# Landmark sums of batch 1 taken from token-layout copies of q and k on TensorE, three subtractions moved to VectorE, and another written order for the first twelve slots

## The chip, the cores and the metric

The kernel runs on one core of a Trainium2 chip. The metric is the device time of one execution in microseconds. Of the kernel before, three timed runs took 854.84, 856.5 and 857.36 us (median 856.5 us); the one execution that was profiled took 852.74 us, of which the trace spans 850.7 us.

## The reference

Three stages follow one another. A Nyström attention over 4 batches, 8 heads, 576 tokens and head size 64; a gated layer on its 2304 x 512 output; and a second layer with a mish-like activation.

```python
q_lm = q.reshape(B, H, m, S // m, D).mean(axis=3)     # m = 32 landmarks, 18 tokens each
k_lm = k.reshape(B, H, m, S // m, D).mean(axis=3)
A, Bm, C = sm(q, k_lm), sm(q_lm, k_lm), sm(q_lm, k)   # scaled softmax rows
Z = Bm.T / (norm1(Bm) * norminf(Bm) + 1e-06)
for _ in range(6):
    Z = 2 * Z - Z @ Bm @ Z
x = A @ Z @ C @ v
...
x = ((x @ w_a) * (x @ w_b)) @ w_out                   # 512 -> 1536 -> 512
...
h = x @ w_in                                          # 512 -> 2048
out = (h * tanh(softplus(h))) @ w_out2
```

The weights arrive as 64-bit floats, and the kernel converts them to 32 bits itself. A landmark is needed as a sum over 18 consecutive tokens; the factor 1/18 is folded into the scale of the exponentials.

## The kernel before

Queries and keys are stored with the head dimension on the partitions (`kt`, `qt`: 128 partitions x 4 head pairs x 576 tokens). `lm_sum` (line 144) makes the landmark sums `kl` and `ql` with one VectorE `tensor_reduce` over two head pairs at a time, so four of them per batch.

For each batch the attention is a chain of small steps that `attention` holds by name: `kl`, `ql`, `sB` (landmark scores and softmax), `BB` and six `NS` (the iteration for Z), `sC0`/`sC1` (landmark queries against all keys, in two halves), `ET0`/`ET1` (transposes), `U` (times v), `M`, and `A0`/`A1`, `A0n`/`A1n` (queries against landmarks, softmax, and a split of the result `af` into a high part and a low part, both in `at`). Each step is a generator that pauses where it goes from one engine to another. The `NS` step asks TensorE, then ScalarE (a copy), then VectorE.

The first layer works in *slots*. A slot is one 128-wide block of hidden columns over 288 tokens: 6 products into one bank for `w_a`, 6 into the next for `w_b` (`ps_ab<-at,bm`, 12 matmul records per slot), a ScalarE copy `ta`, a VectorE product `tg`, and a split `g` on ScalarE and GpSimd. The weights in it are folded first: `fold` multiplies the attention's `MT` with `wab` and splits the result into `bm` (ScalarE copy, VectorE subtraction). The products with `w_out` (`o0` to `o7` in the order, `ps_o<-g,wo`) take 12 matmul records each.

Weight units are converted by `to_f32` (line 367): one ScalarE operation and four VectorE operations on 128 x 512 values. Units `c0` to `c3` give the `wab` for the first fold, `c4` to `c7` for the second, `c8` to `c11` are the first four of `w_out` (they have one more VectorE split, `wo<-f,wo`), `c12` to `c19` come after.

The order of the opening is written out by hand in `ORDER_1` (line 342): each word advances one generator by one pause; a word with `+` belongs to batch 1, a number is that many filler matmuls on an identity, `s0` to `s11` are the first twelve slots, `f0`, `f1`, `F0`, `F1` the folds of batches 0 and 1, `|` the point where banks are handed over. On VectorE, ScalarE and TensorE the words fix the order in which instructions stand; each engine then runs its line strictly in that order. From slot 12 on the order is made by the loops from line 749, which are not changed.

All loads stand in one queue, SP's, in program order. A load into a tile that is in use waits there for its readers. The keys of batch 1 go into the same buffer as those of batch 0 (`tag="kv"`, `bufs=1`), so their load waits until `sC1` of batch 0 has read it.

Of the kernel before, what the change touches and what calls it, by code (L numbers as in the profile page):

```python
# [17 lines left out]
LM = 32  # L18
# [10 lines left out]


@with_exitstack
def nystrom_moe_kernel(ctx: ExitStack, tc: tile.TileContext, q, k, v, w_a, w_b, w_out1, w_in2, w_out2, out):
    nc = tc.nc
    NT = B * S
    gp = nc.gpsimd
# [93 lines left out]
    PAIRS0 = {"sC0": "p3", "ET0": "bm", "ET1": "p3", "A0": "bm", "U": "p3"}  # L129
    PAIRS1 = {"ET0": "bm", "ET1": "bm"}  # L130

    def attention(ap, b, kt, qt, vt0=None):

        x = {}
        first = b == 0
# [2 lines left out]
        def sm(shape, nm, bufs=1, tag=None):  # L138
            return ap.tile(shape, F32, tag=tag or nm, bufs=bufs, name=nm)
# [164 lines left out]
        def An(r):  # L304
            ss, sa = x["ss", r], x["sa"][:, r]
            sa3 = sa.rearrange("p c (n l) -> p (c n) l", l=LM)
            ve.tensor_reduce(out=ss[:, :, 1], in_=sa3, axis=AX, op=ALU.add)
            yield
            ve.tensor_scalar(ss[:, :, 2], ss[:, :, 1], 1e-9, None, op0=ALU.add)
            ve.reciprocal(ss[:, :, 3], ss[:, :, 2])  # L310
            ve.tensor_tensor(sa3, sa3, ss[:, :, 3:4].to_broadcast([128, 18, LM]), op=ALU.mult)
            yield
            af = sm([128, 2, 288], "af")
            for c in range(2):
                ve.transpose(out=af[:, c], in_=sa[:, c])
            yield
            at = AT[b, r] = main.tile([128, 2, 2, S // 2], F32R, tag="AT", bufs=6, name="at")
            ac.activation(at[:, 0], af, AF.Copy)
            yield
            (ve if (b, r) == (0, 0) else gp).tensor_tensor(at[:, 1], af, at[:, 0].bitcast(F32), op=ALU.subtract)  # L320

        steps = {
            "kl": lambda: lm_sum(kt, "kl"), "ql": lambda: lm_sum(qt, "ql"), "sB": sB, "BB": BB, "NS": NS, "U": Uv, "M": M,
# [16 lines left out]

    N_UNITS, N_SLOTS = 20, 12
    ORDER_1 = """
        kl kl ql ql c0 sB sC0 sB c0 sB sC1 4 c1 sB sC0 BB 2 c2 sC1 BB c3 sC1 NS 2 c1 sC1 c2 c3 sC1 c0 c1 NS
        ET0 NS c2 c3 NS 2 ET0 c0 ET1 NS NS c4 c1 A0 ET1 c2 NS 1 c5 A0 U NS c6 NS A0 NS c7 c3 NS A0 NS U NS c0
        NS NS c1 NS NS c2 M A0n M A1 c3 A0n f0 A0n f0 +kl A0n f0 A0n +kl | s0 +ql s0 s0 s1 +ql s1 A1 A1 +sC0
        +sC1 +sC0 A1 +sC1 A1n A1n A1n +sC1 A1n s0 c4 +sC1 A1n s1 c5 c6 +sC1 +sB s1 +sB s0 +ET0 c7 s1 s0 c4 +sB
        s2 +ET0 +sB s1 s2 +ET1 c5 c6 +BB +ET1 c7 c4 s2 c8 +BB +U s2 c5 s2 +NS +U s2 s3 +NS +NS c6 +NS s3 c7 s3
        +NS +NS c4 +NS c5 +NS +NS c6 +NS c7 +NS +NS f1 s3 c8 s3 c8 s3 +NS c8 f1 c8 +NS c9 +NS f1 +NS c8 +NS s4
        c9 +M c9 s4 s4 c9 +M c9 s5 s4 c9 +A0 c8 s5 c9 s4 s5 c10 s4 +A0 s6 s5 F0 c10 s6 c10 s5 +A0 c11 s5 s6 F0
        s7 s6 +A0 c11 +A1 c11 s7 s6 c11 s7 c12 s6 c11 +A0n c11 c11 +A0n +A0n F0 +A0n +A0n s7 F1 c10 s7 c10 s7  # L350
        F1 s8 c12 c12 c10 F1 s8 s8 c10 s9 s8 c12 o0 s9 s8 c12 s8 +A1 c13 s9 +A1 o0 s10 o1 s9 s10 c13 +A1 c13
        s9 c13 c14 s10 s9 c13 o1 s11 s10 c14 s10 o2 c14 s11 s10 c14 c15 c14 s11 o2 c15 c15 o3 +A1n c15 c16
        +A1n o4 o3 c16 c16 o5 c15 o4 c17 +A1n c17 +A1n o6 c17 o5 c16 +A1n c16 o7 o6 s11 c17 s11 s11 c17 c18 o7
        c18 c18 c18 c18 c19 c19 c19 c19 c19
    """

    def stage(src, shape, early):
# [56 lines left out]
                        pass  # L414
                    self.prefetch()

    wab = {}
    wabd = [dram.tile([128, 2048], F32, name=f"wabd{g}") for g in range(6)]

    def wab_units(g):  # L420
        def conv(i, jj, st):
            if g not in wab:
                wab[g] = main.tile([128, 4, 2, 256], F32, tag="wab", bufs=3, name="wab")
            t = wab[g]
            yield from to_f32(t[:, 2 * jj:2 * jj + 2, i], st, True)
# [558 lines left out]
```

## Time and profile before

| | |
|---|---|
| three timed runs | 854.84, 856.5, 857.36 us |
| the profiled execution | 852.74 us, span of its trace 850.7 us |
| PE busy | 794.7 us (93%) |
| DVE busy | 565.8 us (67%) |
| ACT busy | 342.1 us (40%) |
| POOL busy | 153.2 us (18%) |

PE is TensorE's matmuls, PEld its weight loads, DVE is VectorE, ACT ScalarE, POOL GpSimd. The share of busy time is a mean over stages with different limits: in the first two slices of the page's strip (21 us each) PE is at five to six tenths, and from the fifth slice on at nine. DVE runs the other way, with eight and nine tenths at the start and three to four at the end.

An idle time in the trace is put down to the releaser that came last, shown as `[us <-releaser]` behind a row.

### The profile page before, as it was taken

Reading aid. Unit: us, or ns where it says so; the run is one execution under the profiler, and the core shown is the slowest. Engines: PE = TensorE matmul, PEld = TensorE weight load, DVE = VectorE, ACT = ScalarE, POOL = GpSimd, SP = SyncE. Lnnn points to the kernel's source line nnn. Section 1 sums busy time; section 2 is a strip of 40 time slices with the busy share of each in tenths; the row PEclk is TensorE's granted clock in tenths of the full one; section 3 lists DMA queues with packets and bytes.
Section 4 is the critical chain, followed back from the end, with each engine's and each line's share of the span. In section 5 each row is a group of like instructions: output and inputs, shape, how many; then the busy total and the mean of one; then the engine's idle time right before and its main releaser. Section 6 shows DMA issues by size and latency. Waiting matters only on the chain.

```text
span 850.7 us, 14559 instructions
## 1 busy us (share of the span) xinstructions
PE 794.7 (93%) x5802; PEld 691.9 (81%) x5802; DVE 565.8 (67%) x1027; ACT 342.1 (40%) x684; POOL 153.2 (18%) x144
## 2 busy tenths in 40 slices
PE   5666999999999999999988999999999999999997
PEld 4444887987887888787987898988988989988986
DVE  7899977895575488888985678768433347433433
ACT  3335454444323445444443444345332334332332
POOL 0011222222230232122234335320000000000000
PEclk9798899999999999999999899999999999999999
DMA  9736467458227338777376857788655445654501
GB/s 357 306 120 229 160 214 246 179 206 319 81 85 255 163 113 314 247 265 238 115 251 274 302 215 259 264 310 336 247 196 212 173 171 200 227 213 179 186 1 74
DMA packets 47891, 180.85 MB, mean 213 GB/s; under 512 B 4176, under 2 KB 12368, under 8 KB 38480
## 3 DMA queue, kind: packets, MB, share of 16 engines
q1 hardware_dynamic: 47824, 179.93, 58.9%
q8 instruction: 45, 0.74, 0.3%
q14 instruction: 22, 0.18, 0.1%
HBM read 126.44 MB, written 53.48 MB: 211 GB/s over the span
## 4 chain that ended last, share of the span: by engine, by line
PE 75%; DVE 14%; DMA 6%; issue 3%; ACT 2%; SPq 0%; POOL 0%; ACTq 0%; DVEq 0%
PE ps_ab L56 33%; PE ps_o L56 21%; PE ps_bm L56 11%; PE ps_at L56 10%; DVE f L56 5%; DMA kt<-in_k_dram 3%; DMA wi2d<-f 2%; DVE tg L56 1%; DVE f L378 1%; DVE bm L56 1%; DMA wo2d<-f 1%; DVE kl L56 1%; ACT f L374 1%; DVE x2acc L56 1%; DVE s L56 1%
## 5 line engine op out<-in xcount | busy, mean ns | idle before, releaser
L56 PE MATMUL ps_ab<-xc,wc 128*128 128x384 f32 x1008 | 201.7, 340 | 4.8 <-DVE u2s L56 3.1
L56 PE MATMUL ps_ab<-at,bm 128*128 128x288 f32 x1152 | 192.0, 307 | 13.4 <-DVE tg L56 6.9
L56 PEld LDWEIGHTS ps_ab<-at,bm 128*128 128x128 f32 x1152 | 165.4, 194 | 41.9 <-issue 11.8
L56 PEld LDWEIGHTS ps_ab<-xc,wc 128*128 128x128 f32 x1008 | 181.8, 189 | 16.9 <-DVE u2s L56 3.4
L56 PE MATMUL ps_o<-g,wo 128*128 128x288 f32 x1152 | 180.0, 298 | 3.1 <-DVE x2acc L56 2.1
L56 PEld LDWEIGHTS ps_o<-g,wo 128*128 128x128 f32 x1152 | 161.0, 188 | 15.4 <-issue 5.9
L519 POOL TENSOR_TENSOR g<-tg,g 128x288 fp32r<-128x288 f32 x96 | 87.1, 908 | 268.0 <-ACT g L56 268.0
L56 ACT ACTIVATE m<-c 128x384 f32<-128x384 f32 x96 | 50.2, 523 | 189.6 <-DVE c L56 189.5
L56 PE MATMUL ps_bm<-wo,g 128*128 128x512 f32 x288 | 95.5, 396 | 0.3 <-ACT g L56 0.3
L56 PE MATMUL ps_at<-wo,g 128*128 128x512 f32 x288 | 82.9, 395 | 0.0
L56 DVE TENSOR_TENSOR g<-m,g 128x384 fp32r<-128x384 f32 x96 | 66.7, 696 | 23.0 <-ACT g L56 23.0
L56 PE MATMUL ps_o<-wo,g 128*128 128x512 f32 x288 | 79.6, 393 | 0.0
L56 ACT ACTIVATE g<-tg 128x288 fp32r<-128x288 f32 x96 | 42.4, 442 | 79.9 <-DVE tg L56 79.7
L56 DVE SCALAR_TENSOR_TENSOR f<-stg,f 128x512 uint32<-128x512 uint32 x88 | 72.1, 823 | 1.6
L56 PEld LDWEIGHTS ps_at<-wo,g 128*128 128x128 f32 x288 | 54.3, 189 | 10.7
L56 DVE TENSOR_TENSOR tg<-ps_ab,ta 128x288 f32<-128x288 f32 x96 | 43.2, 451 | 29.7 <-PE ps_ab L56 21.9
L56 ACT ACTIVATE ta<-ps_ab 128x288 f32<-128x288 f32 x96 | 38.9, 405 | 57.4 <-PE ps_ab L56 56.9
L56 PEld LDWEIGHTS ps_o<-wo,g 128*128 128x128 f32 x288 | 53.6, 188 | 9.1
L56 PEld LDWEIGHTS ps_bm<-wo,g 128*128 128x128 f32 x288 | 53.7, 189 | 7.0 <-ACT g L56 0.6
L56 ACT ACTIVATE g<-m 128x384 fp32r<-128x384 f32 x96 | 50.3, 523 | 2.6
L56 DVE TENSOR_TENSOR c<-ps_ab,m 128x384 f32<-128x384 f32 x24 | 13.4, 557 | 50.6 <-PE ps_ab L56 50.6
L56 PE MATMUL ps_bm<-wab,mt 64*32 64x512 f32 x384 | 39.3, 644 | 6.2 <-DVE bm L56 6.2
(138 smaller groups left out, 755.1 us busy)
## 6 DMA issues: line engine op xcount, KB each, us to landing
wc<-wcd SPq DMA_DIRECT2D x16, 1792.0 KB, 7.3
wo<-wod SPq DMA_DIRECT2D x16, 1024.0 KB, 4.9
stg<-in_moe_w_out_dram SPq DMA_DIRECT2D x28, 512.0 KB, 4.5
wcd<-wc SPq DMA_DIRECT2D x8, 1792.0 KB, 7.1
wab<-wabd SPq DMA_DIRECT2D x10, 1024.0 KB, 6.3
stg<-in_moe_w_in_dram SPq DMA_DIRECT2D x16, 512.0 KB, 5.1
wod<-wo SPq DMA_DIRECT2D x8, 1024.0 KB, 6.7
stg<-in_moe_w_a_dram SPq DMA_DIRECT2D x12, 512.0 KB, 6.4
```

The costliest lines, as they stand in the source:

```text
L56: i = f(*a, **kw)
L374: i = ac.engine.activation(dst, hi.bitcast(F32), AF.Abs)
L378: i = ve.engine.tensor_scalar(dst, dst, F32_TINY, F32_HUGE, op0=ALU.max, op1=ALU.min)
L519: gp.tensor_tensor(t[:, 1], tg, t[:, 0].bitcast(F32), op=ALU.subtract)
```

## The change

Four edits stand together.

1. The landmark sums of batch 1 leave VectorE. Two more inputs, `q1` and `k1`, hold batch 1 with tokens on the partitions: 126 partitions (7 landmarks of 18 tokens) x 5 groups x 512 columns. `load_tokens` loads each of them in three pieces (1024, 1024 and 512 columns, 1.29 MB in all) into buffers of `x2` and `AT` tiles that are not yet in use; the six loads stand in SP's queue behind `vt` of batch 0 and ahead of the units `c4` to `c7`. `blk` (126 x 7) holds ones where a token belongs to a landmark. A product of 126 x 128 tokens with `blk` gives 7 landmarks of 128 columns; 20 products make `kl`, 20 make `ql`, and one ScalarE copy each brings them into place.
2. The low part of `at` is subtracted on VectorE for both batches and halves; before, only for the first half of batch 0, the other three on GpSimd.
3. `ORDER_1` is another list.
4. The store of a converted `wab` goes out when its fourth unit is done, whichever that is.

```diff
+    blk = const.tile([128, 7], F32, name="blk")
...
+        ve.tensor_reduce(out=blk, in_=ident[:, 0:126].rearrange("p (l k) -> p l k", k=BLK), axis=AX, op=ALU.add)
...
+    def load_tokens():
+        out = []
+        for src in (k1, q1):
+            ts = []
+            for i in range(0, 5, 2):
+                if src is q1 and i:
+                    t = main.tile([128, 2, 2, S // 2], F32R, tag="AT", bufs=6, name="tok").bitcast(F32).rearrange("p a b s -> p (a b s)")
+                else:
+                    t = main.tile([128, 4, 288], F32, tag="x2", bufs=4, name="tok").rearrange("p a s -> p (a s)")
+                w = min(2, 5 - i)
+                nc.sync.dma_start(out=t[0:126, 0:DM * w], in_=src[:, DM * i:DM * (i + w)])
+                ts.append(t)
+            out.append(ts)
+        return out
...
         def lm_sum(src, nm):
             x[nm] = sm([128, 4, LM], nm)
+            if tokens:
+                p, ts = bank("o1"), tokens[nm == "ql"]
+                for j in range(4):
+                    for i in range(5):
+                        n, r = (4, 72) if i == 4 else (7, 126)
+                        f0 = DM * (i % 2) + 128 * j
+                        pe.matmul(p[:, LM * j + 7 * i:LM * j + 7 * i + n], ts[i // 2][0:r, f0:f0 + 128], blk[0:r, 0:n], start=True, stop=True)
+                    yield
+                ac.activation(x[nm].rearrange("p j l -> p (j l)"), p[:, 0:128], AF.Copy)
+                return
...
-            (ve if (b, r) == (0, 0) else gp).tensor_tensor(at[:, 1], af, at[:, 0].bitcast(F32), op=ALU.subtract)
+            (ve if b < 2 else gp).tensor_tensor(at[:, 1], af, at[:, 0].bitcast(F32), op=ALU.subtract)
...
     ORDER_1 = """
-        kl kl ql ql c0 sB sC0 sB c0 sB sC1 4 c1 sB sC0 BB 2 c2 sC1 BB c3 sC1 NS 2 c1 sC1 c2 c3 sC1 c0 c1 NS
+        kl kl ql ql c0 sB sC0 sB c0 sB sC1 4 c1 sC0 sB c2 sC1 BB 2 c2 c3 BB sC1 NS 2 c1 sC1 c0 c1 sC1 c2 c1 NS
...
-            if (i, jj) == (1, 1):
+            converted[g] = converted.get(g, 0) + 1
+            if converted[g] == 4:
                 nc.sync.dma_start(out=wabd[g], in_=t.rearrange("p j i f -> p (j i f)"))
...
     vt0 = load_v(ap, 0)
+    tokens = load_tokens()
     u0.prefetch(8)
     run0 = attention(ap, 0, kt, qt, vt0)
-    run1 = attention(ap, 1, *load_qk(ap, 1))
+    run1 = attention(ap, 1, *load_qk(ap, 1), None, tokens)
```

On VectorE, at the end of batch 0's first attention half: `af` transposes, `kl` and `ql` are the landmark sums of batch 1, `bm` the subtraction of the first fold, `at` the low part, `stC` the maxima of `sC`. Before:

```order
L56 STREAM_TRANSPOSE af<-sa 128x288 x2
L56 TENSOR_REDUCE kl<-kt 128x64
L56 TENSOR_TENSOR bm<-ps_bm,bm 128x1024
L56 TENSOR_TENSOR at<-af,at 128x576
L56 TENSOR_REDUCE kl<-kt 128x64
L56 TENSOR_REDUCE ql<-qt 128x64 x2
L56 STREAM_TRANSPOSE sa<-ps_at 128x288 x2
```

The same place now; `wab` are conversions of the units `c2` to `c7`:

```order
L56 STREAM_TRANSPOSE af<-sa 128x288 x2
L56 SCALAR_TENSOR_TENSOR wab<-stg,wab 128x2x256 x2
L56 TENSOR_TENSOR at<-af,at 128x576
L405 TENSOR_SCALAR wab<-wab 128x2x256 x3
L56 TENSOR_SCALAR wab<-wab 128x2x256
L405 TENSOR_SCALAR wab<-wab 128x2x256
L56 TENSOR_SCALAR wab<-wab 128x2x256 x2
L56 TENSOR_TENSOR bm<-ps_bm,bm 128x1024
L56 SCALAR_TENSOR_TENSOR wab<-stg,wab 128x2x256
L56 STREAM_TRANSPOSE sa<-ps_at 128x288 x2
```

The four reductions are gone from here; `at` stands ahead of `bm`, and seven conversion steps stand between them.

On TensorE, from the last `NS` of batch 0 to the first slot (`rz` is the iterate, `zd,U` is `M`, `wab,mt` the first fold, `qt,kl` the second half of `A`, `at,bm` the slots). Before:

```order
L56 MATMUL ps_at<-rz 32x64 x16
L56 MATMUL ps_at<-rz 32x32 x8
L56 MATMUL ps_at<-zd,U 64x128 x2
L56 MATMUL ps_at<-qt,kl 32x288 x8
L56 MATMUL ps_bm<-wab,mt 32x512 x8
L56 MATMUL ps_ab<-at,bm 128x288 x18
```

Now (`blk,tok` are the landmark products, `o_443` for `kl` and `o_494` for `ql`):

```order
L56 MATMUL ps_at<-rz 32x32 x8
L56 MATMUL ps_o_494<-blk,tok 128x7 x4
L56 MATMUL ps_o_494<-blk,tok 128x4
...
L56 MATMUL ps_at<-zd,U 64x128 x2
L56 MATMUL ps_o_443<-blk,tok 128x7 x4
L56 MATMUL ps_o_443<-blk,tok 128x4
L56 MATMUL ps_bm<-wab,mt 32x512 x8
...
L56 MATMUL ps_at<-qt,kl 32x288 x8
L56 MATMUL ps_ab<-at,bm 128x288 x18
```

Fifteen of the 40 landmark products stand ahead of this piece, among the last `NS` steps; the other 25 stand in it, 15 of them ahead of the fold and all ahead of the first slot.

In SP's queue, behind the first four weight units. Before:

```order
L123 DMA vt<-in_v_dram 128x1560
L123 DMA vt<-in_v_dram 128x1040
L364 DMA stg<-in_moe_w_a_dram 128x2x512
L364 DMA stg<-in_moe_w_b_dram 128x2x512
...
L109 DMA qt<-in_q_dram 128x2304
L364 DMA stg<-in_moe_w_out_dram 128x1024 x3
L109 DMA kt<-in_k_dram 128x2304
```

Now:

```order
L140 DMA vt<-in_v_dram 128x1560
L140 DMA vt<-in_v_dram 128x1040
L125 DMA tok<-in_k_dram 126x1024 x2
L125 DMA tok<-in_k_dram 126x512
L125 DMA tok<-in_q_dram 126x1024 x2
L125 DMA tok<-in_q_dram 126x512
L391 DMA stg<-in_moe_w_a_dram 128x2x512
...
L111 DMA qt<-in_q_dram 128x2304
L391 DMA stg<-in_moe_w_out_dram 128x1024 x3
L111 DMA kt<-in_k_dram 128x2304
```

Six loads more stand ahead of `c4` to `c7` and of the keys of batch 1.

## Rows read from the trace of the kernel before

**Rows 1.** The page: busy time, share of the span, instructions.
```profile
PE 794.7 (93%) x5802; PEld 691.9 (81%) x5802; DVE 565.8 (67%) x1027; ACT 342.1 (40%) x684; POOL 153.2 (18%) x144
```
**Rows 2.** Windows: length, busy us (instructions) of each engine, granted clock, DMA share, GB/s.
```profile
24.55:36.87 12.32, 5.10 (x93) 2.15 (x86) 10.49 (x24) 3.03 (x7) 0.00 (x0) 0.79 1.01 398
36.87:84.92 48.05, 31.70 (x430) 23.37 (x430) 44.55 (x96) 19.63 (x44) 8.15 (x9) 0.86 0.44 158
84.92:111.04 26.12, 26.12 (x187) 22.46 (x187) 25.54 (x43) 12.83 (x26) 7.92 (x7) 0.91 0.59 186
111.04:140.00 28.96, 27.08 (x205) 23.30 (x204) 22.27 (x41) 15.75 (x34) 5.84 (x6) 1.00 0.73 246
140.00:240.00 100.00, 98.22 (x870) 84.45 (x868) 72.10 (x147) 39.96 (x87) 25.25 (x27) 0.98 0.51 180
```
**Rows 3.** Timeline of PE: start, length, count, idle time before and its releaser.
```profile
36.87 4.45 PE L56 MATMUL ps_ab<-at,bm 128*128 128x288 f32 x17 [2.69 <-DVE at L56]
...
84.92 1.96 PE L56 MATMUL ps_bm<-wab,mt 64*32 64x512 f32 x16 [5.69 <-DVE bm L56]
...
108.26 2.94 PE L56 MATMUL ps_o<-g,wo 128*128 128x288 f32 x21
```
**Rows 4.** Timeline of DVE, the sums of batch 1 and what stands between.
```profile
33.66 1.35 DVE L56 TENSOR_REDUCE kl<-kt 128x64 f32<-128x1152 f32 x1 [1.56 <-DMA kt<-in_k_dram]
34.93 1.22 DVE L56 TENSOR_TENSOR bm<-ps_bm,bm 128x1024 fp32r<-128x1024 f32 x1
36.06 0.75 DVE L56 TENSOR_TENSOR at<-af,at 128x576 fp32r<-128x576 f32 x1
36.73 1.34 DVE L56 TENSOR_REDUCE kl<-kt 128x64 f32<-128x1152 f32 x1
37.99 2.60 DVE L56 TENSOR_REDUCE ql<-qt 128x64 f32<-128x1152 f32 x2
40.51 0.84 DVE L56 STREAM_TRANSPOSE sa<-ps_at 128x288 f32<-128x288 f32 x2
```
**Rows 5.** Timeline of DVE, the product of the twelfth slot.
```profile
108.94 0.45 DVE L56 TENSOR_TENSOR tg<-ps_ab,ta 128x288 f32<-128x288 f32 x1
```
**Rows 6.** Timeline of POOL, two of its subtractions for at.
```profile
47.98 1.66 POOL L320 TENSOR_TENSOR at<-af,at 128x576 fp32r<-128x576 f32 x1 [45.98 <-ACT at L56]
...
106.63 1.85 POOL L320 TENSOR_TENSOR at<-af,at 128x576 fp32r<-128x576 f32 x1 [7.48 <-ACT at L56]
```
**Rows 7.** Timeline of DVE, conversions alone and beside a POOL subtraction.
```profile
15.76 1.09 DVE L378 TENSOR_SCALAR wab<-wab 128x512 f32<-128x512 f32 x3
...
47.63 2.29 DVE L378 TENSOR_SCALAR wab<-wab 128x512 f32<-128x512 f32 x3
...
59.37 1.28 DVE L56 SCALAR_TENSOR_TENSOR wab<-stg,wab 128x512 uint32<-128x512 uint32 x2
...
106.51 2.51 DVE L56 SCALAR_TENSOR_TENSOR wab<-stg,wab 128x512 uint32<-128x512 uint32 x2
```
**Rows 8.** Timeline of PE and PEld, filler matmuls with the shape of a landmark product's weights.
```profile
7.48 2.90 PE L56 MATMUL ps_o<-kl,ident 128*128 128x128 f32 x12 [7.48 <-DVE kl L56]
...
11.89 0.97 PEld L56 LDWEIGHTS ps_o<-ident 128*128 128x128 f32 x8 [0.46 <-PE ps_p L56]
```
**Rows 9.** Timeline of ACT and SP: conversions that wait for their load; the keys' load.
```profile
14.47 0.66 ACT L374 ACTIVATE wab<-stg 128x512 f32<-128x512 f32 x1 [0.65 <-DMA stg<-in_moe_w_b_dram]
...
24.01 0.68 ACT L374 ACTIVATE wab<-stg 128x512 f32<-128x512 f32 x1 [0.45 <-DMA stg<-in_moe_w_b_dram]
```
**Rows 10.** Timeline of PE: the score products of batch 1.
```profile
41.45 0.91 PE L56 MATMUL ps_at<-kt,ql 64*32 64x288 f32 x16
```
**Rows 11.** Waits of DVE from 4 to 109 us, summed: time, times, longest.
```profile
DVE rz L56 <- ACT rz L56: 1.5, 3, 0.9
DVE sa L56 <- PE ps_bm L56: 1.2, 1, 1.2
```

More of the change, by code (lines that the diff above doesn't have):

```diff
@@ L31, in nystrom_moe_kernel @@
 @with_exitstack
-def nystrom_moe_kernel(ctx: ExitStack, tc: tile.TileContext, q, k, v, w_a, w_b, w_out1, w_in2, w_out2, out):
+def nystrom_moe_kernel(ctx: ExitStack, tc: tile.TileContext, q, k, v, w_a, w_b, w_out1, w_in2, w_out2, q1, k1, out):
     nc = tc.nc
@@ L130, in nystrom_moe_kernel, with attention @@
     PAIRS1 = {"ET0": "bm", "ET1": "bm"}
-    def attention(ap, b, kt, qt, vt0=None):
+    def attention(ap, b, kt, qt, vt0=None, tokens=None):
         x = {}
@@ L342, in nystrom_moe_kernel @@
     ORDER_1 = """
-        kl kl ql ql c0 sB sC0 sB c0 sB sC1 4 c1 sB sC0 BB 2 c2 sC1 BB c3 sC1 NS 2 c1 sC1 c2 c3 sC1 c0 c1 NS
[L344 to L352, printed above, removed]
@@ L353, in nystrom_moe_kernel @@
-        +A1n o4 o3 c16 c16 o5 c15 o4 c17 +A1n c17 +A1n o6 c17 o5 c16 +A1n c16 o7 o6 s11 c17 s11 s11 c17 c18 o7
-        c18 c18 c18 c18 c19 c19 c19 c19 c19
+        kl kl ql ql c0 sB sC0 sB c0 sB sC1 4 c1 sC0 sB c2 sC1 BB 2 c2 c3 BB sC1 NS 2 c1 sC1 c0 c1 sC1 c2 c1 NS
+        ET0 NS c1 NS 2 ET0 c2 ET1 NS NS A0 c2 ET1 c3 NS 1 A0 U NS NS A0 NS U +kl NS A0 c3 NS +kl c3 c3 NS A0n
+        +kl NS c4 NS A0n NS +ql c5 NS A0n +ql c6 c0 A0n M c0 +kl M A0n c7 c6 f0 +kl c7 c4 c6 +ql f0 c5 c4 c5
+        +ql f0 A1 +ql c5 | s0 A1 s0 s0 A1 s1 s0 A1 +sC0 c4 s1 s1 A1n s0 s0 +sC0 +sC1 A1n +sC1 A1n +sC1 A1n s1
@@ new lines, in nystrom_moe_kernel @@
+        c7 +sC1 A1n c6 +sC1 +sB c7 c8 +sB +ET0 c7 +sB s1 s2 +sB +ET0 s1 s2 s2 c4 c5 +BB s2 +ET1 +BB s2 s3 s2
+        +ET1 c6 +NS s3 +U c8 +NS +NS c8 c8 c9 c8 +NS s3 +U +NS c8 +NS f1 c9 s3 c9 s3 +NS c8 f1 s3 c9 +NS c10
+        +NS f1 +NS +NS +NS s4 c10 c10 c9 +NS s4 s4 +NS +NS c9 c10 +NS s4 s5 +NS s4 s4 c9 s5 s5 c10 c11 +M s5
+        s6 c10 c11 +M c11 s5 +A0 c10 s6 s5 c12 c11 s6 c11 s7 s6 c11 +A0 F1 s7 s6 c11 s7 s6 F1 +A0 o0 F1 +A0 o1
+        o0 +A0n +A0n F0 o1 +A0n o2 s7 F0 c12 c12 +A0n F0 +A1 c13 +A0n s7 o3 c13 o2 c12 s7 c13 c12 c14 s8 c13
@@ L355, in nystrom_moe_kernel @@
+        o3 o4 s8 c14 c13 c14 +A1 s8 o4 c14 s9 s8 o5 c14 s9 s8 +A1 c15 s8 s9 o5 c15 +A1 s10 c15 s9 c16 c15 o6
+        s10 c16 s9 c16 s9 c15 s10 c17 c16 o6 s11 c17 s10 o7 c17 s11 c16 s10 s10 c17 s11 +A1n o7 +A1n c18 s11
+        c18 s11 c18 s11 c17 +A1n c19 c18 +A1n c19 +A1n c19 c19 c18 c19
     """
@@ L415, in step @@
                     self.prefetch()
-    wab = {}
+    wab, converted = {}, {}
     wabd = [dram.tile([128, 2048], F32, name=f"wabd{g}") for g in range(6)]
@@ L975 @@
         args.append(nc.dram_tensor(f"in_{name}_dram", a.shape, _mybir.dt.from_np(a.dtype), kind="ExternalInput").ap())
+    for name in "qk":
+        a = _np.pad(inputs[name].reshape(B, H, S, D)[1].transpose(1, 0, 2).reshape(S, DM), ((0, 54), (0, 0)))
+        a = arrays[f"in_{name}1_dram"] = _np.ascontiguousarray(a.reshape(5, 126, DM).transpose(1, 0, 2)).reshape(126, 5 * DM)
+        args.append(nc.dram_tensor(f"in_{name}1_dram", a.shape, _mybir.dt.from_np(a.dtype), kind="ExternalInput").ap())
     for i, (shape, dtype) in enumerate(_OUTS):
```

## The prediction

> **What bounds the kernel now.** I read the page first, then a table of windows, then the timelines of PE and DVE beside each other, and at the end the waits. The page has PE busy for 93% and DVE for 67% of the span [rows 1], which says too little: the table of windows shows who leads where [rows 2]. From 36.87 to 84.92 us PE is busy 31.70 of 48.05 us and DVE 44.55; from 84.92 to 111.04 PE is busy all of 26.12 us, and from 140 to 240 us 98.22 of 100. So the opening is paced by DVE, and behind about 85 us the kernel is a full line of matmuls. Whatever lets PE reach a given matmul of that line earlier is kept to the end, as long as nothing empties the line later. The change touches only work ahead of slot 12.
>
> Within the opening the reader should see two places. At 36.87 us the first slots had waited for `at` on DVE [rows 3], which stood behind a landmark sum that itself had waited 1.56 us for the keys' load [rows 4]. At 84.92 us PE had waited 5.69 us for a `bm` subtraction [rows 3], again DVE's turn and not a slow operation. DVE runs strictly in its line, so I keep its account up to one place that both orders share: the product `tg` of the twelfth slot, which DVE starts at 108.94 us [rows 5]. Up to there the matmul line of either order holds the same work to within a few products: the row at 108.26 [rows 3] takes the output products to 105 records at 145 slot records; the new order has 102 at 144.
>
> **The change part by part**, as a sum on DVE's line up to that `tg`.
>
> *The sums that go.* Four reductions of batch 1, from start to start: 33.66 to 34.93 is 1.27, 36.73 to 37.99 is 1.26, 37.99 to 40.51 is 2.52 [rows 4]. Together -5.05 us. With the first of them goes its wait for the keys, -1.56 us [rows 4].
>
> *The subtraction of `at`.* It took 0.67 us on DVE from 36.06 to 36.73 [rows 4]. Two of the three that move to DVE stand ahead of the twelfth `tg`, the third behind: +1.34. The new order also has one conversion step more ahead of that place (0.64, half of the pair that took 1.28 [rows 7]) and leaves two transposes behind it (the pair took 0.84 [rows 4]). Together +1.14.
>
> *What POOL no longer disturbs.* While POOL ran its `at` from 47.98 to 49.64 [rows 6], three DVE conversions took 2.29 us; the same three took 1.09 with POOL idle: 1.20 lost [rows 7]. At 106.63 [rows 6] a pair of the last conversion step took 2.51 in place of 1.28: 1.23 lost [rows 7]. The third shares its stretch with a `g` subtraction that stays; I give it half, 0.6. Together -3.0. The bounds are 0, if the `g` subtractions move into the gap and disturb DVE as much, and 1.66 + 1.85 and the mean of the two, 1.76, so -5.3, if DVE had stood still for all of POOL's time. I take the measured pairs.
>
> The Trainium skill's page "SBUF — State Buffer", section "Who interferes with whom", calls the shared port of DVE and GpSimd an exclusive lock, held for a whole instruction. The trace agrees that a DVE instruction stops beside POOL, but the rows show 1.20 of 1.66 us; with the lock's full length the sum below would be 2.3 us larger.
>
> *What PE takes over.* 40 fp32 products, which the trace records in two passes each, as it does the fillers: 80 weight loads of 128 x 128 with at most 7 columns behind each. No row has that shape. The nearest is the fillers' weight load at full clock, eight in 0.97, so 0.121 each [rows 8]: 80 x 0.121 = 9.7 us. They stand between `U` and the first slots, where PE is idle 12.32 - 5.10 = 7.2 us [rows 2]. So 2.5 us would stand on the path: the fold, its `bm` and the second half of `A` come that much later. Bounds: 0, if they fit into the idle time; and at the low clock's price of the whole filler, twelve in 2.90, 0.242 each [rows 8], 19.3 us, or 12.1 beyond the idle time. I take 2.5, since the weight load is what remains of the filler when its 128 columns shrink to 7. They also keep PE busy ahead of the first slots, whose 17 matmuls took 4.45 us [rows 3]; I count nothing for it, because `kl` and `ql` and then DVE were later than they.
>
> *What the loads push back.* Units 4 and 8 of the staging queue were waited for at 14.47 and 24.01 us [rows 9]; between them lie four units of 0.52 MB and `vt` of 1.33 MB, 3.43 MB in 9.54 us, so 0.36 MB/us. The six token loads, 2.58 MB, take 7.2 us of that line. `c7` then lands at about 31.2 us and holds ScalarE's line, in which the copy for `bm` stands next but one; that copy is over by about 33.5 us, ahead of the 34.93 at which DVE reached `bm` before [rows 4]. The keys land at about 33.6 + 7.2 = 40.8, and PE needs them at 41.45 [rows 10]. So I count 0 for the loads; that cover is 0.7 us thick, and each microsecond beyond costs one, since slot products and `sC1` stand behind `sC0` on PE.
>
> The Trainium skill's page "DMA: Bandwidth & Descriptors", section "Why a DMA increments its semaphore by 16 and not by 1", says that a DMA uses the largest number of engines up to 16 that divides its outer dimension: 14 for 126 rows. As an estimate from that page the tokens would take 8.2 us and the keys land at 41.8, which takes about 0.4 us from the gain. No row here shows such a load.
>
> *The rest at nothing.* `blk` is made while DVE waits for the first keys; two ScalarE copies of 128 x 128 fall where ACT is busy 3.03 of 12.32 us [rows 2]; the store of `wab` moves by less than a unit.
>
> Sum: -5.05 - 1.56 + 1.14 - 3.0 + 2.5 = -5.97, so **6.0 us less**. The profiled execution took 852.74 us and would take 846.8; the median of the three runs, 856.5, becomes 850.5 us. What is late next is DVE still: behind the twelfth `tg` the third `at` subtraction comes back (0.67), and PE, which had 1.9 us idle from 111.04 to 140 [rows 2], could idle a little more there.
>
> **The rivals.**
>
> *A, the forecast*: DVE paces the opening as before, and the account holds. 847 to 854, chance 0.46.
>
> *B, more*: the other waits go as well. For it speaks that the list has the output products ahead of the last four slots, so that PE need not stand idle as at 84.92. DVE's waits for the iteration and for `A`, 1.5 + 1.2 [rows 11], and the 2.5 us of landmark products, if they fit into idle time, would come on top: 6.0 + 5.2 = 11.2, so 845. Against it: these waits are latencies of a chain that is still there. Chance 0.25.
>
> *C, nothing or little*: the keys land late. If the line of loads ran at 0.32 instead of 0.36 MB/us with the tokens in it, they would land at 40.8 x 0.36 / 0.32 = 45.9 us, 4.4 beyond PE's need, and the gain would be 1.6: 854.9. For it speaks that the DMA share in that stretch is 1.01 [rows 2], so nothing can be hidden there; against it, that the rate stood at 398 GB/s. Chance 0.18.
>
> *D, slower*: the landmark products at the low clock. At 0.242 each they put 12.1 us on the path in place of 2.5, and the sum becomes +3.6: 860. It decides from 0.196 us a record on (8.5 us beyond the idle time use up the rest of the sum). For it: the granted clock was 0.79 over that stretch [rows 2], so part of it ran at 1.2 GHz; against it: that was with PE idle more than half of the time, and now the products fill it. Chance 0.11.
>
> **How the numbers follow.** The likeliest is A, 850.5 us. The range from 843 to 858.5 takes in B with 2 us beyond it and stops short of D. A measurement of this kernel tells a difference from 0.3%, 2.6 us, so from 853.9 down it counts as faster and from 859.1 up as slower. Faster: nearly all of A (0.44), B (0.25), half of C (0.09), so 0.78. Slower: most of D, 0.09. The same: 0.13.
>
> **What would show it.** In the changed kernel's profile: no DVE reduction `kl<-kt` at 33 us; `blk,tok` records at about 0.12 us from start to start, and the clock near 1 among them; the first full run of slots at 36 to 38 us; the keys' load landed by 42 us; conversions near the two `at` places at 0.36 and 0.64 us each; the twelfth `tg` at about 103 us; PE without the 5.69 us gap. It is wrong if the twelfth `tg` comes at 108 us or later, if PE waits for `kt` or for the tokens, or if PE gives the gain back in waits for DVE between 105 and 140 us.

## The result and the profile after

The changed kernel took 847.04 us (845.6 to 847.71, four runs) beside 855.67 us (854.74 to 857.36) for the kernel before: a ratio of 0.9895, 95% interval 0.9872 to 0.9917. Run again among the experiments, it was 846.78 beside 853.14 us: 0.9929 [0.9906, 0.9952]. So it is 6 to 9 us faster. The forecast was 850.5 us from a median of 856.5, so 6.0 less. The size came out, by luck: most of the way to it did not.

The profiled execution took 847.19 us, its trace spans 845.1. The busy line of the page, against [rows 1]:

```profile
PE 803.3 (95%) x5882; PEld 702.7 (83%) x5882; DVE 553.7 (66%) x1027; ACT 343.6 (41%) x686; POOL 147.8 (17%) x141
```

DVE has 12 us less to do and PE 9 us more. The first three windows of [rows 2], of the changed kernel (length, busy us of PE, PEld, DVE, ACT and POOL, granted clock, DMA share, GB/s):

```profile
24.55:36.87 12.32, 12.03 (x90) 11.33 (x89) 7.56 (x19) 3.77 (x8) 0.00 (x0) 0.56 1.04 338
36.87:84.92 48.05, 38.10 (x464) 28.17 (x463) 37.05 (x87) 18.73 (x45) 6.08 (x6) 0.76 0.64 237
84.92:111.04 26.12, 26.12 (x213) 21.77 (x205) 25.71 (x49) 13.17 (x27) 4.46 (x5) 1.00 0.62 202
```

In the first of them PE went from 5.10 to 12.03 us of work, and the granted clock fell from 0.79 to 0.56. In the second DVE is no longer full: 37.05 where it had 44.55. The timeline of PE shows what fills the first (start, length, shape, count, idle time before and its releaser):

```profile
23.86 1.06 PE L56 MATMUL ps_o<-blk,tok 126*128 126x7 f32 x8
25.21 1.91 PE L56 MATMUL ps_o<-blk,tok 72*128 72x4 f32 x12 [0.29 <-DMA tok<-in_k_dram]
...
27.63 2.29 PE L56 MATMUL ps_o<-blk,tok 126*128 126x7 f32 x10
...
30.22 4.43 PE L56 MATMUL ps_o<-blk,tok 126*128 126x7 f32 x20
...
35.21 2.30 PE L56 MATMUL ps_o<-blk,tok 126*128 126x7 f32 x10
...
39.33 4.43 PE L56 MATMUL ps_o<-blk,tok 126*128 126x7 f32 x20
43.68 1.21 PE L56 MATMUL ps_at<-qt,kl 64*32 64x288 f32 x16
46.25 0.85 PE L56 MATMUL ps_ab<-at,bm 128*128 128x288 f32 x2 [1.35 <-ACT bm L56]
47.51 3.51 PE L56 MATMUL ps_ab<-at,bm 128*128 128x288 f32 x16 [0.41 <-DVE bm L56]
50.94 0.72 PE L56 MATMUL ps_at<-kt,ql 64*32 64x288 f32 x16
```

Eight landmark records take 1.06 us, 0.13 each; twenty take 4.43, 0.22 each. The 80 together take 16.4 us. Three windows of the same kernel say why:

```profile
23.86:25.20 1.34, 1.06 (x15) 0.97 (x8) 1.31 (x5) 0.80 (x2) 0.00 (x0) 1.00 1.03 261
...
30.20:34.60 4.40, 4.40 (x30) 4.36 (x22) 2.81 (x7) 1.55 (x3) 0.00 (x0) 0.50 1.07 405
...
39.30:43.70 4.40, 4.40 (x31) 4.36 (x23) 0.00 (x0) 0.00 (x0) 0.00 (x0) 0.50 0.95 395
```

The first records run at a granted clock of 1.00 (2.4 GHz), the others at 0.50 (1.2 GHz), though PE does not stand still from 25.21 to 44.9 us. The last window has something else: DVE and ACT do nothing for 4.4 us. ACT's timeline has:

```profile
35.69 0.66 ACT L401 ACTIVATE wab<-stg 128x512 f32<-128x512 f32 x1
45.00 0.28 ACT L56 ACTIVATE kl<-ps_o 128x128 f32<-128x128 f32 x1 [8.65 <-PE ps_at L56]
45.18 1.02 ACT L56 ACTIVATE bm<-ps_bm 128x1024 fp32r<-128x1024 f32 x1
```

And DVE's, with the twelfth `tg` below:

```profile
46.23 1.23 DVE L56 TENSOR_TENSOR bm<-ps_bm,bm 128x1024 fp32r<-128x1024 f32 x1 [7.46 <-ACT bm L56]
...
111.00 0.45 DVE L56 TENSOR_TENSOR tg<-ps_ab,ta 128x288 f32<-128x288 f32 x1
```

The copy of batch 1's `kl` needs the one `kl` buffer, and batch 0's `A1` (`ps_at<-qt,kl`, 43.68) still has to read the old one, behind the 80 records of landmark products. The copy for `bm` stands behind it on ACT, and DVE waits 7.46 us for that. The first slots come at 46.25 where [rows 3] have 36.87, and the twelfth `tg` at 111.00 us, later than 108.94 [rows 5].

So where is the gain? Three points of PE's line hold the same work in both kernels: the first score product of batch 1 (`ps_at<-kt,ql`, [rows 10]), the fold after the iteration of batch 2, and the first product of the second layer. The last two on PE's timeline of before:

```profile
193.11 1.09 PE L56 MATMUL ps_bm<-wab,mt 64*32 64x512 f32 x16
...
456.62 2.25 PE L56 MATMUL ps_ab<-xc,wc 128*128 128x384 f32 x12
```

And on that of the changed kernel:

```profile
192.83 1.09 PE L56 MATMUL ps_bm<-wab,mt 64*32 64x512 f32 x16
...
454.61 2.25 PE L56 MATMUL ps_ab<-xc,wc 128*128 128x384 f32 x12
```

They cut the span into four pieces, I to IV. The table has them for every kernel that ran (start of the `kt,ql` row, the differences of the starts, and the span less the last start), with the time's ratio to the kernel before:

| kernel | I, to `kt,ql` | II, to the fold | III, to layer 2 | IV, to the end | ratio [95%] |
|---|---|---|---|---|---|
| before | 41.45 | 151.66 | 263.51 | 394.1 | 1 |
| after | 50.94 | 141.89 | 261.78 | 390.5 | 0.9895 [0.9872, 0.9917] |
| after, again | 52.07 | 140.24 | 261.98 | 389.9 | 0.9929 [0.9906, 0.9952] |
| before + 28 bytes | 42.29 | 149.57 | 267.13 | 390.4 | 0.996 [0.9938, 0.9982] |
| before + 64 bytes | 41.89 | 150.47 | 262.80 | 392.0 | 0.9985 [0.9968, 1.0003] |
| after, `blk` elsewhere | 51.62 | 140.13 | 261.73 | 394.0 | 0.9986 [0.9968, 1.0004] |
| sums on VectorE | 47.70 | 141.10 | 262.49 | 393.6 | 0.9955 [0.9937, 0.9973] |
| the same + 28 bytes | 48.65 | 141.50 | 263.21 | 389.5 | 0.9908 [0.9886, 0.9929] |
| column-tiled products | 52.86 | 139.81 | 265.30 | 390.1 | 0.9976 [0.9956, 0.9996] |
| 128-row tokens | 51.37 | 142.65 | 260.47 | 389.4 | 0.9915 [0.9893, 0.9938] |
| both of these | 52.56 | 144.04 | 263.97 | 389.1 | 0.9927 [0.99, 0.9953] |
| late query products | 50.19 | 142.67 | 262.94 | 389.6 | 0.9897 [0.9867, 0.9928] |
| two `kl` buffers | 48.87 | 141.12 | 261.83 | 389.6 | 0.9908 [0.9881, 0.9936] |
| subtraction on GpSimd | 54.37 | 140.88 | 259.65 | 389.6 | 0.9937 [0.9914, 0.996] |

Before to after: I +9.49, II -9.77, III -1.73, IV -3.6 us. The opening, I and II, gives 0.3 us. The largest piece behind it is the second layer, which the change does not touch. The windows of II, before and after:

```profile
41.45:193.11 151.66, 133.57 (x1248) 111.39 (x1248) 131.53 (x261) 70.58 (x153) 34.49 (x35) 0.95 0.56 192
...
50.94:192.83 141.89, 132.09 (x1250) 110.96 (x1249) 126.27 (x253) 70.01 (x153) 29.02 (x32) 0.96 0.61 205
```

Of the 9.8 us, PE's idle time gives 8.3 (18.1 before, 9.8 after) and its busy time 1.5.

Each row is one execution. Kernels with the same opening show how much that scatters: I + II is 191.8 to 192.8 for the three with after's opening (mean 192.3) and 191.9 to 193.1 for the three with before's (192.4). The traced execution need not be a typical one: of the six runs each of "late query products" (842.4 to 847.36 us) and "both of these" (844.34 to 851.8) it was the slowest, and of those of "two `kl` buffers" (843.23 to 847.09) the fastest.

### The profile page after: what moved, and what is told of

It is laid out like the page before. It is cut to its first block, busy times and chain, and to the rows that moved or that the text cites. A ratio compares the mean times of both kernels' runs of the same rounds, so it can differ in the third digit from the quotient of the medians.

```text
span 845.1 us, 14731 instructions
## 1 busy us (share of the span) xinstructions
PE 803.3 (95%) x5882; PEld 702.7 (83%) x5882; DVE 553.7 (66%) x1027; ACT 343.6 (41%) x686; POOL 147.8 (17%) x141
## 4 chain that ended last, share of the span: by engine, by line
PE 77%; DVE 11%; DMA 6%; issue 3%; ACT 2%; POOL 1%; SPq 0%; DVEq 0%; ACTq 0%
PE ps_ab L56 33%; PE ps_o L56 22%; PE ps_bm L56 11%; PE ps_at L56 11%; DVE f L56 4%; DMA tok<-in_k_dram 2%; DVE f L405 1%; DMA wi2d<-f 1%; DVE tg L56 1%; DMA wo2d<-f 1%; DMA stg<-in_moe_w_a_dram 1%; DMA kt<-in_k_dram 1%; ACT f L401 1%; DVE s L56 1%; DVE bm L56 1%
## 5 line engine op out<-in xcount | busy, mean ns | idle before, releaser
L56 PE MATMUL ps_ab<-at,bm 128*128 128x288 f32 x1152 | 189.9, 306 | 7.5 <-DVE tg L56 5.4
L56 DVE TENSOR_TENSOR g<-m,g 128x384 fp32r<-128x384 f32 x96 | 59.9, 624 | 25.6 <-ACT g L56 25.6
L56 DVE TENSOR_TENSOR u2s<-ps_ab,m 128x384 f32<-128x384 f32 x24 | 13.4, 556 | 45.8 <-PE ps_ab L56 45.8
```

The source lines that it names most:

```text
L56: i = f(*a, **kw)
```

## The experiments

**The place of the tiles.** The new constant `blk` has 28 bytes per partition; what is allocated after it on its side of SBUF lies further by that, counted as 32 bytes with alignment (no run prints an address). Does the second layer's gain come from that?

```diff
+    pad = const.tile([128, 7], F32, name="pad")
...
+        gp.memset(pad, 0.0)
```

> The kernel before with one unused constant tile of 28 bytes per partition beside the others, so that the tiles allocated after it on that side of SBUF lie 32 bytes further, as they do in the changed kernel; no other work but one memset of 7 columns. Theory 1 (the gain is the opening's: less work on VectorE): no change, 855 to 857 us. Theory 2 (the opening nets nothing, and the second layer's faster matmul spacing, 3.7 us of the profiled 5.55, comes from where the tiles lie): 850 to 853 us, with the 384-column products of the second layer at 173.5 ns apart instead of 175.5. Theory 3 (that spacing varies from run to run): no change in the median, and a spacing anywhere between.

And the other way round, the changed kernel with `blk` out of the way:

```diff
-    blk = const.tile([128, 7], F32, name="blk")
...
+    blk = ap.tile([128, 7], F32, tag="blk", bufs=1, name="blk")
```

> The changed kernel with the tile of block ones held in the attention pool, so that the constants, weights and accumulators ahead of it lie where they lie in the kernel before. Theory 1: as the changed kernel, 846 to 848 us. Theory 2: the second layer goes back to the spacing of before, 175.5 ns, and the time to 850 to 853 us. Theory 3: 846 to 848 us with a spacing anywhere between.

Groups of PE's instructions by shape from 620 to 820 us, a stretch in which PE waits for nothing (count | busy us, mean ns | idle). The kernel before:

```profile
L56 PE MATMUL ps_ab<-xc,wc 128*128 128x384 f32 x537 | 106.8, 337 | 0.0
...
L56 PE MATMUL ps_at<-wo,g 128*128 128x512 f32 x150 | 42.8, 394 | 0.0
```

The changed kernel:

```profile
L56 PE MATMUL ps_ab<-xc,wc 128*128 128x384 f32 x543 | 106.9, 335 | 0.0
...
L56 PE MATMUL ps_at<-wo,g 128*128 128x512 f32 x156 | 44.2, 391 | 0.0
```

The kernel before with the 28 bytes:

```profile
L56 PE MATMUL ps_ab<-xc,wc 128*128 128x384 f32 x542 | 106.8, 335 | 0.0
...
L56 PE MATMUL ps_at<-wo,g 128*128 128x512 f32 x154 | 43.7, 391 | 0.0
```

The changed kernel with `blk` elsewhere:

```profile
L56 PE MATMUL ps_ab<-xc,wc 128*128 128x384 f32 x537 | 106.7, 337 | 0.0
...
L56 PE MATMUL ps_at<-wo,g 128*128 128x512 f32 x156 | 44.5, 394 | 0.0
```

Each matmul is 2 to 3 ns shorter where the tiles lie further, with either code. The mean from the start of a 384-column product to the start of the next, over the same stretch, is 175.5 ns before, 173.5 after and with the 28 bytes, 175.4 with `blk` elsewhere. IV is 393.6 to 394.1 us in the three rows at the old place and 389.1 to 390.5 in the ten at the new one, whatever else differs: the groups lie 3.1 us apart and spread by at most 1.4. The idle constant made the kernel before 0.4% faster (849.52 beside 852.32 us), and the changed kernel without the shift is 0.9986, no difference that can be told. So 3.6 us of the gain in the traces is a by-product of 28 bytes. By the times, the two parts 0.996 and 0.9986 multiply to 0.9946; that lies inside the interval of the second comparison and outside that of the first, so these parts do not explain all of the first one's 8.6 us.

The last experiment asks whether any other place does as well.

```diff
+    pad = const.tile([128, 16], F32, name="pad")
```

> The kernel before with an unused constant of 64 bytes per partition, where the 28 bytes of the first experiment (32 with their alignment) took the second layer's 384-column products from 175.5 to 173.5 ns and the time to 0.996. If what counts is where the tiles lie within 64 bytes (an odd multiple of 32 bytes is the faster place): the spacing is back at 175.5 ns and the time at 1.000 of before. If any move away from the old place helps, or a larger one helps more: 173.5 ns or less and 0.996 or less.

The first answer, but not for all products: by shape, the 384-column products are back at the old length (175.8 ns from start to start) and the 512-column ones stay short (227.4 ns, where it is 231.3 before and 229.1 with the 28 bytes). IV is 392.0, and the time cannot be told from before.

```profile
L56 PE MATMUL ps_ab<-xc,wc 128*128 128x384 f32 x541 | 107.7, 337 | 0.0
...
L56 PE MATMUL ps_at<-wo,g 128*128 128x512 f32 x156 | 44.1, 391 | 0.0
```

So the two shapes do not answer to the place in the same way. Which tile against which address is left open.

**Order and subtraction without the products.** The new order, the subtraction on VectorE, and batch 1's sums on VectorE as before; `blk` is gone too, so the tiles lie at the old place:

```diff
-    tokens = load_tokens()
...
-    run1 = attention(ap, 1, *load_qk(ap, 1), None, tokens)
+    run1 = attention(ap, 1, *load_qk(ap, 1))
...
-    ... NS U +kl NS A0 c3 NS +kl c3 c3 NS A0n +kl NS c4 NS A0n NS +ql c5 NS A0n +ql c6 c0 ...
+    ... NS U NS A0 c3 NS c3 c3 NS A0n NS c4 NS A0n NS c5 NS A0n c6 c0 ...
```

> The changed kernel's order and its subtraction on VectorE, with the landmark sums of batch 1 back on VectorE's tree (no token loads, no products, no tile of block ones; the first three key steps and both early query steps are left out of the order). Theory 1 (taking 5.05 us of sums off VectorE pays): 3 to 5 us slower than the changed kernel, 850 to 852 us. Theory 2 (the products cost PE some 16 us at the low clock before the first slots and win nothing there): as fast as the changed kernel in the opening or faster, first slots at 36 to 40 us instead of 46, and 844 to 850 us, the rest depending on the place of the tiles, which is that of before.

Then the same with 28 idle bytes:

> The changed kernel's order and subtraction on VectorE, batch 1's landmark sums on VectorE, and an unused 28-byte constant that puts the tiles where the changed kernel has them. If the two gains add (order and subtraction -4.3 us by the 148th microsecond of the profile, place of the tiles -3.7 us in the second layer): 3 to 4 us faster than the same without the constant, 843 to 845 us, and faster than the changed kernel by 2 to 4 us, which would say that the token copies and their products cost what the rest of the change wins. If they don't add: as the changed kernel, 847.

The first is 0.9955 of before, 847.18 beside 852.32 us. Against the changed kernel at the same place of the tiles (0.9986) it is the faster one: the products and their loads cost, and do not win. The intervals just overlap (0.9973 and 0.9968), but both kernels were timed beside each other on one chip, and there the seven runs of the one (845.54 to 849.83 us, median 847.18) and the twelve of the other (849.58 to 855.01, median 850.74) hardly meet: 3.6 us. The opening says the same: 188.80 us to the fold where the changed order with products has 191.8 to 192.8. With the 28 bytes it is 0.9908, so the gains add, and 190.15 to the fold; beside the changed kernel on the same chip the medians differ by 1.6 us (845.19 and 846.78), which is within the noise. The means of the traces, 189.5 without products and 192.3 with them, put their cost at 2.8 us; order and subtraction together win 2.9 (192.4 before). The PE timeline of the first kernel shows how its opening differs:

```profile
34.16 1.24 PE L56 MATMUL ps_at<-qt,kl 64*32 64x288 f32 x16
...
37.56 0.40 PE L56 MATMUL ps_ab<-at,bm 128*128 128x288 f32 x1 [1.54 <-DVE at L56]
43.56 4.21 PE L56 MATMUL ps_ab<-at,bm 128*128 128x288 f32 x16 [5.60 <-DVE bm L56]
47.70 1.21 PE L56 MATMUL ps_at<-kt,ql 64*32 64x288 f32 x16
```

Three of the four sums stand ahead of `bm` on DVE, PE waits 5.60 us for it, and still the scores of batch 1 start 3.2 us earlier than at 50.94.

**The products' time on PE, and their loads.** The products in four column tiles of 32, as `U` has them:

```diff
+                        for c in range(0, 128, 32):
+                            pe.matmul(p[c:c + 32, ...], ts[i // 2][0:r, f0 + c:f0 + c + 32], blk[0:r, 0:n], ...)
```

> The changed kernel with each landmark product split into four 32-column weight tiles, the form in which the U products ran 80 records in 1.75 us. If what delays the first slots (46.25 us instead of 36.87) is the weight load and product of 0.22 us each on PE: the 80 products fall from some 16 us to 7 or less, and the first slots come 2 to 8 us earlier; by Theory 1 the time falls by as much as the opening gains, 840 to 846 us. If the order's later steps and the loads set the opening (Theory 2's reading of VectorE's waits): the twelfth tg stays at 109 to 111 us and the time within 1 us of 847. Four times as many instructions could also make it slower: 850 us if each costs 0.06 us more.

On its PE timeline:

```profile
25.98 0.72 PE L56 MATMUL ps_o<-blk,tok 126*32 126x7 f32 x65
32.29 0.39 PE L56 MATMUL ps_o<-blk,tok 126*32 126x7 f32 x15 [5.59 <-issue]
...
34.23 0.76 PE L56 MATMUL ps_o<-blk,tok 126*32 126x7 f32 x41
38.48 0.71 PE L56 MATMUL ps_o<-blk,tok 126*32 126x7 f32 x39 [3.50 <-issue]
```

Here 41 records take 0.76 us, 0.019 each, but the line stops for 5.59 and 3.50 us with no releaser (`issue`), and a third time for 1.17 us at 44.05, and the first slots come at 47.46. The expectation of 7 us or less was right for the products and wrong for what follows: the time, 0.9976, is worse than the changed kernel's. It is the 850 us that the expectation gave for instructions that cost more each, but not for that reason. Then the loads. From 20 to 28 us the kernel before moves 406 GB/s and the changed kernel 246:

```profile
20.00:28.00 8.00, 5.73 (x170) 3.86 (x168) 6.59 (x18) 3.87 (x10) 0.00 (x0) 0.91 1.03 406
...
20.00:28.00 8.00, 7.71 (x173) 6.10 (x171) 6.45 (x16) 2.00 (x6) 0.00 (x0) 0.88 1.04 246
```

The next edit gives the token copies two more rows, of zeros that nothing reads:

```diff
-                nc.sync.dma_start(out=t[0:126, 0:DM * w], in_=src[:, DM * i:DM * (i + w)])
+                nc.sync.dma_start(out=t[:, 0:DM * w], in_=src[:, DM * i:DM * (i + w)])
```

> The changed kernel with the token-layout copies of queries and keys held and loaded as 128 rows instead of 126 (two rows more of zeros, which no product reads). Theory L (the 126-row transfers slow all transfers beside them: 240 to 250 GB/s from 20 to 28 us where the kernel before moves 390 to 420): the rate goes back to about 400, the stage loads land some 5 us earlier, the first slots come 0 to 3 us earlier (then PE's 0.22 us per product still holds them), time 844 to 847 where the changed kernel has 847. Rival (the new inputs' place in memory or the mix of transfers is slow, not the row count): the rate stays at 250 and so does the time.

The same window of this kernel:

```profile
20.00:28.00 8.00, 8.00 (x155) 5.94 (x155) 5.51 (x15) 1.82 (x6) 0.00 (x0) 0.75 1.05 393
```

The row count is the cause of the slow loads: 393 GB/s with 128 rows, 246 with 126. The Trainium skill's page "DMA: Bandwidth & Descriptors", section "Why a DMA increments its semaphore by 16 and not by 1", gives 14 engines for 126 rows; as an estimate from it the rate would fall to 14/16, or 344. The trace has far less, so the page's rule does not give the size; how many engines carried these loads no view shows, and the DMA share stays at 1.04. Yet the opening won nothing (first slots at 46.02, fold at 194.02), nor can the time be told from the changed kernel's (845.46 and 846.78 us on one chip): the loads were hidden. Both edits together, on PE's timeline below the expectation:

> 128-row token copies and each landmark product in four 32-column weight tiles, so that both the loads and PE are relieved. If loads and PE's product time each hold the first slots by themselves at 44 to 47 us (the tiled products alone moved them from 46.25 to 47.51 us, waiting for loads): together they come at 37 to 41 us, the opening gains 3 to 6 us by the 148th microsecond, time 841 to 845 us. If ScalarE's copy of the key landmarks (8.65 us of wait) and the vector work hold them: under 2 us, 845 to 847. If the row count doesn't matter: 847 to 850 as the tiled kernel.

```profile
32.78 0.31 PE L56 MATMUL ps_o<-blk,tok 126*32 126x7 f32 x15 [3.63 <-issue]
...
38.97 0.71 PE L56 MATMUL ps_o<-blk,tok 126*32 126x7 f32 x39 [3.67 <-issue]
```

Nothing against the changed kernel (0.9927 beside 0.9929), though it does better than the tiled products with 126 rows (0.9976), which were timed on another chip. PE stops at the same three instructions, after 65, 41 and 28 records of a run, with the loads at 1.6 times the rate; so it isn't the tokens that it waits for. The trace's DMA packets say what it is. One queue, `q8 instruction`, carries instructions in packets of 16384 bytes. In the two tiled kernels the three stops end 1.2 to 1.4 us behind the end of such a packet (30.99, 37.19 and 42.84 us for stops that end at 32.29, 38.48 and 44.05 in the first), and from stop to stop PE's line has 256 instructions each time. So PE had run out of instructions: the tiled products have four times as many as the whole ones, and they were done faster than they were loaded. That is read from times that go together, not from a run that moved the packets, and what made the packets late is open.

**What stands between the products and batch 1.** First the buffer:

```diff
-            x[nm] = sm([128, 4, LM], nm)
+            x[nm] = sm([128, 4, LM], nm, 2 if nm == "kl" else 1)
```

> The changed kernel with a second buffer for the key landmarks and nothing else, so that ScalarE's copy of batch 1's (which waits 8.65 us for batch 0's last reader on PE) holds up neither itself nor the copy of bm behind it. If this wait is part of what delays the first slots: bm is copied at 40 us instead of 45.18, VectorE's 7.5 us wait shrinks to 2 or less, the first slots start at 45 instead of 46.25 and 47.51, 1 to 2.5 us gained, 844 to 846 us. If PE's products alone bind: no change, 847 us.

On PE's timeline:

```profile
43.95 1.21 PE L56 MATMUL ps_at<-qt,kl 64*32 64x288 f32 x16
45.09 3.85 PE L56 MATMUL ps_ab<-at,bm 128*128 128x288 f32 x18
48.87 0.71 PE L56 MATMUL ps_at<-kt,ql 64*32 64x288 f32 x16
```

And on DVE's:

```profile
40.82 1.23 DVE L56 TENSOR_TENSOR bm<-ps_bm,bm 128x1024 fp32r<-128x1024 f32 x1 [2.23 <-ACT bm L56]
```

The slots now follow `A1` without a wait, and DVE waits 2.23 us for that `bm` in place of 7.46. From the start of `A1` to batch 1's scores it takes 4.92 us, where the three traces with after's opening have 7.3 to 8.0 (50.94 - 43.68 in the first): 2.3 to 3.0 us, in the very stretch that the buffer acts on. The fold comes at 189.99, 2.3 us ahead of the changed kernel's mean. The time, 845.25 beside 853.83 us, cannot be told from the changed kernel's by its interval. So by this one trace most of the products' 2.8 us is the one buffer; in the time it is not resolved.

Then the query products behind the first slots, with two `kl` buffers and 128-row tokens:

```diff
-  U +kl NS A0 c3 NS +kl c3 c3 NS A0n +kl NS c4 NS A0n NS +ql c5 NS A0n +ql c6 c0 A0n M c0 +kl M A0n c7 c6 f0 +kl c7 ...
+  U +kl NS A0 c3 NS +kl c3 c3 NS A0n +kl NS c4 NS A0n NS +kl c5 NS A0n +kl c6 c0 A0n M c0 M A0n c7 c6 f0 c7 ...
+  ... f0 A1 +ql +ql c5 | s0 A1 s0 +ql s0 A1 s1 +ql s0 A1 +ql +sC0 ...
```

> The changed kernel with 128-row token copies, two buffers for the key landmarks, and the order changed: the key products take the five earliest places, the 40 query products go behind the first A1 step and between the first slots (where PE stood idle 4 of 8 us from 52 to 60 us). Theory P (the 80 products at 0.22 us each, on PE ahead of the first slots at the low clock, are what eats the opening's gain): first slots at 38 to 42 us instead of 46.25, the opening 2 to 4 us ahead of the changed kernel by the 148th microsecond, time 842 to 845 us. Rival (what VectorE and ScalarE still have to do binds the twelve slots whenever the products run): first slots earlier, but the lead is gone by the twelfth tg and the time is that of the changed kernel, 846 to 848 us.

On PE's timeline:

```profile
41.78 1.79 PE L56 MATMUL ps_ab<-at,bm 128*128 128x288 f32 x6
...
50.19 0.72 PE L56 MATMUL ps_at<-kt,ql 64*32 64x288 f32 x16 [0.37 <-ACT ql L56]
```

The first slots came 4.5 us earlier than in the changed kernel, and the fold at 192.86, where it was; the twelfth `tg` at 110.96 us had lost the lead, as the rival says. So in the trace the rival holds: the start of the first slots is not what counts. The time does not bear it out: the median, 844.13 us, lies in the range of theory P (842 to 845) and not in the rival's (846 to 848), and the traced execution was the slowest of the six, so between the two it stays undecided. The table says what goes with the end of the opening: in the eleven rows with the new order, II is 139.8 to 144.0 us whatever happens ahead; in the three with the old one it is 149.6 to 151.7. The fold follows the start of batch 1's scores, to within that spread. The interval of the time's ratio, 0.9897, overlaps that of the changed kernel.

**The subtraction of `at`** back on GpSimd:

```diff
-            (ve if b < 2 else gp).tensor_tensor(at[:, 1], af, at[:, 0].bitcast(F32), op=ALU.subtract)
+            (ve if (b, r) == (0, 0) else gp).tensor_tensor(at[:, 1], af, at[:, 0].bitcast(F32), op=ALU.subtract)
```

> The changed kernel with the subtraction of the attention tiles back on GpSimd, all but the first. The prediction's account gives the move to VectorE -3.0 us (GpSimd no longer disturbs VectorE's conversions) and +1.14 us (its own time): by it this kernel is about 2 us slower than the changed one, 848 to 850 us. If the gain of the order comes without this part: 846.5 to 847.5 us. If VectorE's own time for it is what counts: 845 to 846 us.

848.31 us, 0.9937 where the changed kernel has 0.9929: not told apart. In its trace the fold is at 195.25, 3.0 us behind the changed kernel's mean, but it was 2.3 to 2.8 us behind at the first slots already (48.98), ahead of the first subtraction that moved. (1.56 us of that is a stop like those above, in the products of `U`: it ends at 25.28, 1.4 us behind the end of an instruction packet. So an opening can come out later by more than the three traces above differ.) That leaves 0.2 to 0.7 us for the edit, less than the scatter; the account had 1.9.

## Why the prediction came out, step by step

*That DVE paces the opening* was read rightly for the kernel before and did not outlive the change. The prediction said it was wrong if the twelfth `tg` came at 108 us or later; it came at 111.00. Of its other signs, the records came at 0.22 us in place of 0.12, the first full run of slots at 47.51 in place of 36 to 38, and the keys landed at 45.1 in place of 42 or earlier. DVE's work did shrink, and then DVE waited, 7.46 us in one place. The number is right by luck.

*What PE takes over* is the term that failed. The 0.121 us a record was right at the full clock (0.13 measured) and wrong for the stretch: most of the records ran at a granted clock of 0.50 and took 0.22 us, as rival D had it. All 80 took 16.4 us in place of 9.7, so 9.2 us beyond the idle time in place of 2.5, and the prediction's own sum with that is 0.7 us slower and not 6.0 faster. (The 0.242 us that it called the low clock's price is from 7.48 to 10.38 us, ahead of that trace's first record of the clock at 11.2; the low clock's price was first shown by the changed kernel.) The prediction held against D that the products fill PE's idle time. They filled it, 12.03 of 12.32 us, and the granted clock was 0.56 where it had been 0.79 with 5.10 us of work.

*The rest at nothing* hid a second failure. The two ScalarE copies were counted by ACT's free time, but the copy of `kl` waited 8.65 us for the buffer that `A1` had still to read, with the copy for `bm` and then DVE behind it. A second buffer took 2.3 to 3.0 us off that stretch.

*What D missed*, and the prediction too: the new order needs 9.8 us less from batch 1's first scores to the fold (II); that it is the order and not the subtraction the last variant shows, with 140.88 us and the subtraction back on GpSimd. With output products ahead of the last slots PE has no 5.69 us wait as in [rows 3], and from 84.92 to 111.04 it is full at a clock of 1.00 where it had 0.91; that wait is 5.69 of the 8.3 us by which PE's idle time fell. Rival B had named that; it paid for what D took. The 2.9 us that order and subtraction win and the 2.8 that the products cost leave nothing.

*The sums and the wait for keys*, -5.05 and -1.56, are gone from DVE as counted and bought no time: with the sums back on DVE the kernel is faster by 3.6 us at the old place of the tiles and not slower at the new one. The prediction's terms for this exchange, -5.05, -1.56 and +2.5, make -4.1 us; the traces have +2.8.

*POOL's disturbance*, -3.0 and +1.14: not resolved in time, 0.2 to 0.7 us in the trace.

*The loads at nothing* was right, and the numbers beneath it wrong: 246 GB/s in place of 360 (0.36 MB/us), `c7` converted at 35.69 instead of landed at 31.2. The keys landed at 45.1 us, close to rival C's 45.9 and behind the 41.45 that the prediction allowed; it cost nothing, because batch 1's scores were later still (50.94).

*The 6 us themselves* (5.6 between the two traces) come from two places that no step names: the second layer, 3.6 us, shown by adding the shift to the one kernel and taking it from the other to be the place of the tiles; and III, 1.7 us in this pair of traces. III runs the same code in all kernels and goes from 259.7 to 267.1 without following any edit, so that part is put down to no edit and its cause is open.

## What to carry to other kernels

A new constant moves every tile behind it: compare a stretch that the change does not touch, instruction by instruction, before any of the gain is put down to the edit, and try the idle constant alone. Price matmuls that are new to a stretch at both of TensorE's clocks; a busy PE was no proof of the high one here. And before work is moved to an idle engine, look for the single buffer through which its result passes: here one trace puts 2.3 of 2.8 us down to one `kl` tile. Count instructions too: a product cut into four is four times the instructions to load.

## What was not expected of the hardware

- A constant of 28 bytes ahead of them changes the spacing of the second layer's 384-column products by 2 ns in 175.5, and the stage of 394 us by 3.6 us; 64 bytes change the 512-column ones alone.
- 126 rows in place of 128 in six loads took all that moved between 20 and 28 us, those loads among it, from 393 to 246 GB/s, with the share of busy DMA time unchanged (1.05 and 1.04).
- A run of 126 x 32 weight tiles with 7 columns each goes at 0.019 us a record, faster than instructions come: PE stopped 1.2 to 5.6 us at fixed instructions, each time until 1.2 to 1.4 us after a packet of 16384 bytes of instructions had ended.
